# A fused recurrent-attention, expert and gated feed-forward kernel: two of eight pre-narrowed up-weight tiles move to the last stage, its second and third token groups start sooner, and its weight loads change queue

## The chip, the cores and the metric

The kernel runs on one core of a Trainium2 chip, in one launch. The metric is device microseconds (us) of one execution. Engines: PE (TensorE), DVE (VectorE), ACT (ScalarE), POOL (GpSimd) and SP (SyncE, which here only issues transfers). Each engine runs its instructions in the order in which they were written for it; semaphores tie the engines together.

## The reference

Three layers follow each other over 3072 tokens. The first is a gated recurrent attention (4 batches, 8 heads, 768 steps, head size 40), which gives rows of 320. The second sends each row to one of eight experts. The third, which the change is about, normalises each row and runs a gated feed-forward of width 1536:

```python
rms = np.sqrt(np.mean(x * x, axis=-1, keepdims=True) + 1e-06)
xn = x / rms * rms_g
g = xn @ w_gate                      # 320 -> 1536
silu = g * (1.0 / (1.0 + np.exp(-g)))
val = xn @ w_val                     # 320 -> 1536
return (silu * val @ w_out).astype(np.float32)
```

The weights of the third layer arrive as 64-bit floating point numbers.

## The kernel before, in words

**Stages.** Attention runs until about 220 us of the span, the expert stage from there to about 434 us, and the last stage to the end. All of it is written for the engines in one fixed order (`manual_schedule`), so the order below is the order on each engine.

**Number form.** Matmuls take 16-bit floats. A value is split into a high and a low 16-bit part, and products of the parts are summed. Weights of the last stage must first be *narrowed*: a 64-bit number is turned into a 32-bit one by five DVE instructions (`narrow`, L1263 to L1267, on 384 columns for an up tile and 320 for a down tile), ACT then scales it and rounds it to the high part, and the difference is the low part.

**Expert stage.** 28 blocks of 128 gathered rows. For block j, `xpose` (L1078) turns the gathered rows on the SP queue, `up` makes 16 matmuls (L1110), ACT and DVE split the result into h, SP turns h (L1118), and `down` makes 24 matmuls (L1142). The block after next is gathered by POOL. Beside this, `ffn_jobs` narrows some of the up weights of the last stage for later: per job one SP load (L1279, 384 KB), five DVE instructions, ACT and DVE for the two parts (L1294, L1301) and a store of the narrowed tile to DRAM (`UWS`, L1307). `UF` says how many of the 12 up tiles are done here, two jobs each (gate and value). `due` at L1162 says in which block each step of job k is written: its load in block 2 + floor(6k/5), and the rest in the four blocks behind. SP takes a job's load after the two turns of h, ahead of the next turn of x.

**Last stage.** Tokens come in six groups of 512 (n = 0 to 5), the up weights in 12 tiles (f). A *slot* is `upf(n, f)`: 16 matmuls of 128x512 into two PSUM banks (L1484), tanh on ACT (`th`, L1488), two DVE instructions (`u`, L1494 and L1495), the high part on ACT (`h`, L1499) and the low part on POOL (L1500). PSUM holds three slots: the banks of slot p are used again by slot p + 3. `plan` (L1531) is the list of slots: first groups 0, 1, 2 over the tiles f < UF, then f from UF on with the three groups in turn, then group 3 until its seventh tile, then the down matmuls of group 0 (`downf(0)`, L1517), and so on. With UF = 8 group 1 starts at slot 8, group 2 at slot 16, and `downf(0)` comes behind slot 42.

**A token group** is made ready in eight steps, placed beside slots by `beside` (L1538): step 5 `fetch` (four POOL gathers, L1334), steps 6 and 7 the sums of squares on ACT (L1349), with the norm on DVE and POOL (L1355, L1356) and the token numbers on POOL (L1361) behind 7, then steps 0 to 3: for 128 rows each, ACT scales (L1372, L1374), POOL subtracts (L1375) and copies (L1380), and SP turns the rows into `XT` (L1391).

**Narrowing in the last stage.** The other up tiles (f >= UF, eight jobs with UF = 8) and all 12 down tiles are narrowed beside the slots: `fill` is one list of small steps, seven to a job (five DVE steps, `high` on ACT, `low` on POOL), and each slot takes an equal share of the list (`at`), from slot 2 to slot 42, half ahead of the slot's two `u` instructions and half behind its `h`. The raw weights have three buffers; `low` of job k also issues the load of job k + 3 (`wload`, L1412), here on SP.

Of the kernel before, what the change touches and what calls it, by code (L numbers as in the profile page):

```python
# [11 lines left out]
I32 = mybir.dt.int32  # L12
# [23 lines left out]
OO = DM + H * 41  # L36
NEG = -1.0e30
FJ = (23, 24, 25)
UF = 8
HB = 43  # L40
TS = ((0, 7),), ((1, 1), (2, 3), (3, 5))
PARK = {6: 4, 4: 5, 5: 7}
# [32 lines left out]
class Net:  # L75
# [38 lines left out]
    def consts(self):  # L114
# [30 lines left out]
        self.MP = dp.tile([32, 3, S], BF, name="MP")  # L145
        self.UWS = dp.tile([UF, 128, 2, 5 * 128], F16, name="UWS")

# [940 lines left out]
    def moe(self):  # L1088
        nc, M, P = self.nc, self.M, self.P
# [69 lines left out]
        due = {}  # L1159
        for k, job in enumerate(jobs):  # L1160
            for step, (late, part) in zip(job, ((0, 1), (2, 0), (2, 1), (3, 0), (3, 1), (4, 0))):
                steps = due.setdefault((6 * k // 5 + late, part), [])  # L1162
                steps.insert(len(steps) * part, step)
        w2 = self.w2
        slot = [0]
# [77 lines left out]
    def ffn_weights(self):  # L1243
        self.UW = self.up.tile([128, NF, 2, 5, 128], F16, name="UW")
        self.XT = [self.up.tile([128, 4, 6, 128], F16, name=f"XT{i}") for i in range(4)]
        for f in range(UF):
            self.uw(f)
# [22 lines left out]
    def ffn_jobs(self):  # L1270
# [3 lines left out]
        def job(f, g):  # L1274
            st = {}

            def load():
                t = st["t"] = self.stg().bitcast(I32)
                nc.sync.dma_start(t[:, 0:768], self.i["wu"][f, g].bitcast(I32))  # L1279

            def some(lo, hi):
                def go():
                    if lo == 0:
                        st["v"], st["steps"] = self.narrow(st["t"], 384)
                    for step in st["steps"][lo:hi]:
                        step()

                return go

            def high():  # L1290
                of = st["of"] = st["t"][:, 0:320].bitcast(F16)
                for k in range(3):
                    c = slice(128 * k, 128 * k + 128)
                    nc.scalar.activation(of[:, c], st["v"][:, c], AF.Copy, scale=self.gs[:, k : k + 1])  # L1294

            def low():
                v, of = st["v"], st["of"]
                for k in range(3):
                    c, p = slice(128 * k, 128 * k + 128), slice(64 if k == 2 else 0, 128)
                    out = of[p, c] if k == 2 else of[:, 384 + 128 * k : 512 + 128 * k]  # L1300
                    nc.vector.scalar_tensor_tensor(  # L1301
                        out=out, in0=v[p, c], scalar=self.gs[p, k : k + 1], in1=of[p, c],
                        op0=ALU.mult, op1=ALU.subtract,
                    )

            def store():
                nc.scalar.dma_start(self.UWS[f, :, g], st["of"])  # L1307

            return load, some(0, 2), some(2, 5), high, low, store

        return [job(f, g) for f in range(UF) for g in range(2)]

# [82 lines left out]
    def ffn(self):  # L1395
        nc, F, P = self.nc, self.F, self.P
# [6 lines left out]
        fetch, norm1, norm2, flip = self.fetch, self.norm1, self.norm2, self.flip  # L1403
        todo = [(f, g) for f in range(UF, NF) for g in range(2)] + [(f, None) for f in range(NF)]
        raw = {}

        def wload(k):
            if k < len(todo):
                f, g = todo[k]
                src = self.i["wo"][128 * f : 128 * f + 128] if g is None else self.i["wu"][f, g]  # L1410
                t = F.tile([128, 768 + 384], F32, tag="wraw", bufs=3, name="wraw").bitcast(I32)
                nc.sync.dma_start(t[:, 0 : 2 * src.shape[-1]], src.bitcast(I32))  # L1412
                raw[k] = t

        def wjob(k):

            f, g = todo[k]
            st = []

            def narrow(i):  # L1420
                if i == 0:
                    st.extend(self.narrow(raw.pop(k), DM if g is None else 384))
                st[1][i]()

            def high():
                v = st[0]
                if g is None:
                    nc.scalar.activation(DW[:, f, 0], v, AF.Copy, scale=WSC)
                    nc.scalar.activation(v, v, AF.Copy, scale=WSC)
                    return  # L1430
                for i in range(3):
                    c = slice(128 * i, 128 * i + 128)
                    nc.scalar.activation(v[:, c], v[:, c], AF.Copy, scale=self.gs[:, i : i + 1])
                nc.scalar.activation(UW[:, f, g, 0:3].rearrange("p k c -> p (k c)"), v, AF.Copy)

            def low():
                v = st[0]
                sub = lambda out, a, b: nc.gpsimd.tensor_tensor(out, a, b, ALU.subtract)  # L1438
                if g is None:
                    sub(DW[:, f, 1], v, DW[:, f, 0])  # L1440
                else:
                    two = lambda a: a.rearrange("p k c -> p (k c)")
                    sub(two(UW[:, f, g, 3:5]), v[:, 0:256], two(UW[:, f, g, 0:2]))
                    tail = UW[64:128, f, g, 2]
                    sub(tail, v[64:128, 256:384], tail)
                wload(k + 3)

            return [lambda i=i: narrow(i) for i in range(5)], high, low
# [3 lines left out]
        for k in range(len(todo)):  # L1452
            n, high, low = wjob(k)
# [76 lines left out]
        run = lambda n, a, b: [(n, f) for f in range(a, b)]  # L1530
        plan = [x for n in range(3) for x in run(n, 0, UF)]  # L1531
        plan += [(n, f) for f in range(UF, NF) for n in range(3)]
        plan += run(3, 0, 7) + [(0,)] + run(3, 7, NF) + [(1,)] + run(4, 0, 3) + [(2,)]
# [1 line left out]
        order = [x for x in plan if len(x) == 2]  # L1535
        beside = {(0,): [[(4, 6)], [(4, 7), (4, 0)], [(4, 1), (4, 2)], [(4, 3)]]}
        beside[2,] = [[(5, k) for _, k in ks] for ks in beside[0,]]
        for n, p, steps in ((1, 0, (6, 7, 0, 1, 2, 3)), (2, 5, (5, None, None, 6, 7, 0, 1, 2, 3)), (3, 18, (5, None, None, 6, 7, 0, 1, 2, 3))):  # L1538
            for i, k in enumerate(steps):
                if k is not None:  # L1540
                    beside.setdefault(order[p + i], []).append((n, k))
        beside[3, 0], beside[3, 7] = [(4, 5)], [(5, 5)]
        fetch(1)
        for k in range(3):
            wload(k)
# [101 lines left out]
```

## Time and profile before

| what | value |
|---|---|
| time of three runs | 815.86 us median (813.55, 815.86, 821.99) |
| the profiled execution | 818.5 us, of which its span is 816.7 us |
| PE, DVE, ACT, POOL busy | 95%, 54%, 44%, 46% of the span |
| granted TensorE clock, mean | 0.963 of full speed |
| expert stage | from about 220 us to 434 us |
| last stage | from 434.25 us to the end |

The profile is one execution. "Busy" is the time in which an engine had an instruction in it, also one that was held up after its start. A wait is the idle time ahead of an instruction, with what ended it. PE is busy for 95% of the span, so the waits of PE, and what ends them, say where time can come from or go to. For the other engines the shares are averages over three stages with different work; the rows below give the last stage by itself.

### The profile page before, as it was taken

How to read it: one execution, taken by the hardware profiler on the slowest of the kernel's cores; microseconds unless marked ns; L12 is line 12 of the kernel's file. 1: busy time of each engine (PE TensorE's matmuls, PEld its weight loads, DVE VectorE, ACT ScalarE, POOL GpSimd, SP SyncE). 2: the span in 40 equal slices, each digit the busy share in tenths (PEclk: the TensorE clock that was granted, in tenths of full speed). 3: DMA queues.
4: the chain of work that ended last, by engine and by line, in shares of the span. 5: the costliest groups of instructions: out<-in, count | busy, mean ns of one | idle time of the engine just before them, and what ended most of it. 6: DMA issues, size and time to landing. Idle time of an engine off the chain costs nothing. (4 is left out here: it accounts for less than half of the span.)

```text
span 816.7 us, 15414 instructions
## 1 busy us (share of the span) xinstructions
PE 772.0 (95%) x5288; PEld 491.0 (60%) x5288; DVE 437.1 (54%) x874; ACT 357.8 (44%) x775; POOL 375.0 (46%) x445
## 2 busy tenths in 40 slices
PE   8999999998689999999899998999999999999993
PEld 7799998987245555555455444444565575544662
DVE  7658988885874645465223877778712112243010
ACT  4557878773422333233425664554432232233110
POOL 3537877862563323223424885765634232233221
PEclk9879999996889999999999999999999999999997
DMA  6567877864579999999875432242121020000000
GB/s 198 162 211 233 275 238 253 262 206 149 160 156 199 228 232 228 208 204 233 173 131 209 91 88 62 73 83 61 49 71 41 25 64 17 25 0 1 25 17 25
DMA packets 135573, 109.60 MB, mean 134 GB/s; under 512 B 107287, under 2 KB 116127, under 8 KB 135497
## 3 DMA queue, kind: packets, MB, share of 16 engines
q1 hardware_dynamic: 123561, 87.33, 43.5%
q0 software_dynamic: 5408, 13.83, 6.0%
q10 hardware_dynamic: 6528, 7.44, 2.9%
q8 instruction: 48, 0.79, 0.4%
q14 instruction: 28, 0.23, 0.1%
HBM read 67.59 MB, written 16.82 MB: 103 GB/s over the span
## 5 line engine op out<-in xcount | busy, mean ns | idle before, releaser
L1484 PE MATMUL gv<-XT,UW 128*128 128x512 f16 x1152 | 249.8, 379 | 2.8 <-DMA XT<-xr 2.8
L1484 PEld LDWEIGHTS <-UW 128*128 128x128 f16 x1152 | 112.7, 98 | 137.9 <-issue 3.2
L1494 DVE SCALAR_TENSOR_TENSOR u<-th,gv 128x512 f32<-128x512 f32 x72 | 49.4, 686 | 156.7 <-ACT th L1488 154.1
L1500 POOL TENSOR_TENSOR h<-u,h 128x512 f16<-128x512 f32 x72 | 84.8, 1180 | 105.4 <-ACT h L1499 104.9
L1517 PE MATMUL do<-DW,h 128*128 128x320 f16 x864 | 118.5, 299 | 0.9 <-POOL DW L1438 0.9
L1110 PE MATMUL ups<-W,xt 128*128 x448 | 105.8, 391 | 12.6 <-DMA xt<-xg 11.6
L1517 PEld LDWEIGHTS <-h 128*128 128x128 f16 x864 | 84.5, 98 | 34.8 <-issue 1.1
L1499 ACT ACTIVATE h<-u 128x512 f16<-128x512 f32 x72 | 45.4, 630 | 112.9 <-DVE u L1495 112.9
L1114 ACT ACTIVATE h<-ups 128x512 f16<-128x512 f32 x56 | 33.4, 597 | 124.9 <-PE ups L1110 103.5
L1142 PEld LDWEIGHTS <-hT 128*128 128x128 f16 x672 | 66.2, 99 | 32.5 <-issue 2.1
L1110 PEld LDWEIGHTS <-xt 128*128 128x128 f16 x448 | 44.8, 100 | 67.1 <-DMA xt<-xg 14.2
L1115 DVE SCALAR_TENSOR_TENSOR h<-ups,h 128x512 f16<-128x512 f32 x56 | 38.6, 691 | 85.2 <-ACT h L1114 43.9
L1070 POOL DMA_INDIRECT xg<-XD,IDX x28 | 28.8, 1029 | 97.9 <-DMA xt<-xg 92.8
L1522 POOL DMA_INDIRECT out_dram<-os,TKN x24 | 23.5, 980 | 80.2 <-ACT os L1520 76.7
L1495 DVE SCALAR_TENSOR_TENSOR u<-u,gv 128x512 f32<-128x512 f32 x72 | 49.5, 688 | 14.6 <-PE gv L1484 10.3
L488 PE MATMUL S<-QK 104*128 104x128 f32 x384 | 53.4, 284 | 1.7 <-DMA QK<-in_pqk_dram 1.7
L544 PEld LDWEIGHTS Y<-t,D 128*128 128x128 f32 x352 | 52.6, 204 | 3.7 <-issue 0.3
L544 PE MATMUL Y<-t,D 128*128 128x41 f32 x352 | 54.3, 259 | 0.0
L488 PEld LDWEIGHTS S<-QK 104*128 104x128 f32 x384 | 52.0, 201 | 3.3 <-issue 2.6
L1142 PE MATMUL dps<-W2A,hT 128*128 x336 | 51.2, 301 | 2.0 <-ACTq L1224 2.0
L1142 PE MATMUL dps<-W2B,hT 128*128 x336 | 51.6, 303 | 0.0
L1488 ACT ACTIVATE th<-gv 128x512 f32<-128x512 f32 x72 | 42.3, 587 | 17.0 <-PE gv L1484 17.0
(274 smaller groups left out, 1139.3 us busy)
## 6 DMA issues: line engine op xcount, KB each, us to landing
t<-in_pk_dram SPq DMA_DIRECT2D x22, 484.0 KB
QK<-in_pqk_dram SPq DMA_DIRECT2D x48, 160.0 KB
stg<-in_wu_dram SPq DMA_DIRECT2D x16, 384.0 KB
stg<-in_w_dram SPq DMA_DIRECT2D x9, 640.0 KB
XD<-xr SPq DMA_DIRECT2D x23, 192.0 KB
YD<-LG ACTq DMA_DIRECT2D x26, 160.5 KB
stg<-in_w_dram SPq DMA_DIRECT2D x8, 512.0 KB
wraw<-in_wo_dram SPq DMA_DIRECT2D x12, 320.0 KB
```

The lines of the kernel that those rows point to most:

```text
L488: nc.tensor.matmul(ps[:, i * L : (i + 1) * L], t["kz"][:, j, i], t["t1"][:, i], start=True, stop=True)
L544: nc.tensor.matmul(t["Y"][:, hp, 41 * hf : 41 * hf + 41], t["D"][hf][:, hp * L : (hp + 1) * L], t["vv"][:, 4 * hf + hp], start=False, stop ...
L1110: nc.tensor.matmul(ps, t["xt"][:, kx], self.W1[:, ds(o1 + (kw * F1 + f * 512), 512)], start=(n == 0), stop=(n == 7),)
L1115: nc.vector.scalar_tensor_tensor(out=h[:, 1], in0=ps, scalar=0.0, in1=h[:, 0], op0=ALU.max, op1=ALU.subtract)
L1142: nc.tensor.matmul(ps[:, 0:DM], hT[:, l, k % 4], r, start=(n == 0), stop=(n == 23))
L1484: nc.tensor.matmul(ps, UW[:, f, gv, kw], xt[:, :, 3 * hl + kx], start=(a == 0), stop=(a == 7))
L1488: nc.scalar.activation(th, pg, AF.Tanh, scale=0.5 / (XN * WSC))
L1494: nc.vector.scalar_tensor_tensor(out=u, in0=th, scalar=1.0, in1=pg, op0=ALU.add, op1=ALU.mult)
L1495: nc.vector.scalar_tensor_tensor(out=u, in0=u, scalar=1.0 / (XN * WSC) ** 2, in1=pv, op0=ALU.mult, op1=ALU.mult)
L1499: nc.scalar.activation(hh, u, AF.Copy)
L1500: nc.gpsimd.tensor_tensor(hl, u, hh, ALU.subtract)
L1517: nc.tensor.matmul(ps[:, 0:DM], l[:, s], DW[:, f, w], start=(a == 0), stop=(a == 3 * NF - 1))
```

## The change

Four edits: `UF` goes from 8 to 6, so 12 jobs instead of 16 are narrowed in the expert stage, and 24 instead of 20 in the last stage (12 up, 12 down; half of the 24 up jobs). The expert stage's jobs are spread as 2 + floor(3k/2). The loads of `wload` go from SP to POOL. And the steps of groups 1 and 2 are placed sooner, since group 1 now starts at slot 6 and group 2 at slot 12: group 1 has steps 6 and 7 at slot 0, 0 and 1 at slot 1, 2 at slot 2, 3 at slot 3; group 2 has its fetch at slot 2 and its last step at slot 9 (before: 5 and 13).

```diff
-UF = 8
+UF = 6
...
-                steps = due.setdefault((6 * k // 5 + late, part), [])
+                steps = due.setdefault((3 * k // 2 + late, part), [])
...
-                nc.sync.dma_start(t[:, 0 : 2 * src.shape[-1]], src.bitcast(I32))
+                nc.gpsimd.dma_start(t[:, 0 : 2 * src.shape[-1]], src.bitcast(I32))
...
-        for n, p, steps in ((1, 0, (6, 7, 0, 1, 2, 3)), (2, 5, (5, None, None, 6, 7, 0, 1, 2, 3)), (3, 18, (5, None, None, 6, 7, 0, 1, 2, 3))):
+        for n, p, steps in ((1, 0, (6, 0, 2, 3)), (1, 0, (7, 1)), (2, 2, (5, None, 6, 7, 0, 1, 2, 3)), (3, 18, (5, None, None, 6, 7, 0, 1, 2, 3))):
```

What this does to the order of instructions is shown at three places. The first is POOL at the start of the last stage, from the gathers of group 1 (`yg`) on. In a row stand the line, the operation, the tile written and those read. `h` is the low part of a slot, `nrm` the norm, `xr` the rows of a group, `UW` a narrowed up tile, `wraw` a raw weight. Before:

```order
L1334 DMA yg<-YD,RSLOT 128x321 x4
L1500 TENSOR_TENSOR h_5767<-u_5763,h_5766 128x512
L1500 TENSOR_TENSOR h_5797<-u_5793,h_5796 128x512
L1356 TENSOR_TENSOR nrm<-nrm,NH 128x4
L1361 COPY TKN<-yg 128x1 x4
L1375 TENSOR_TENSOR xr_5828<-yg,xr_5828 128x320
L1380 COPY xr_5828<-xr_5828 128x2x64
L1500 TENSOR_TENSOR h_5839<-u_5834,h_5838 128x512
L1375 TENSOR_TENSOR xr_5864<-yg,xr_5864 128x320
L1380 COPY xr_5864<-xr_5864 128x2x64
L1500 TENSOR_TENSOR h_5875<-u_5870,h_5874 128x512
```

Now (the rows from the third load on down to the last 128 rows of group 1):

```order
L1412 DMA wraw<-in_wu_dram 128x768 x3
L1500 TENSOR_TENSOR h_5709<-u_5705,h_5708 128x512
L1356 TENSOR_TENSOR nrm<-nrm,NH 128x4
...
L1375 TENSOR_TENSOR xr_5749<-yg,xr_5749 128x320
L1380 COPY xr_5749<-xr_5749 128x2x64
L1500 TENSOR_TENSOR h_5759<-u_5755,h_5758 128x512
L1375 TENSOR_TENSOR xr_5782<-yg,xr_5782 128x320
L1380 COPY xr_5782<-xr_5782 128x2x64
L1500 TENSOR_TENSOR h_5794<-u_5788,h_5793 128x512
L1334 DMA yg<-YD,RSLOT 128x321 x4
L1375 TENSOR_TENSOR xr_5827<-yg,xr_5827 128x320
L1380 COPY xr_5827<-xr_5827 128x2x64
```

Three loads now stand behind the gathers of group 1, and the four gathers of group 2 stand ahead of the last rows of group 1; before they stood behind them.

The second place is POOL some slots later, where only slots (`h`) and up tiles are left. Before:

```order
L1500 TENSOR_TENSOR h_6328<-u_6323,h_6327 128x512
L1438 TENSOR_TENSOR UW<-wraw,UW 128x256
L1438 TENSOR_TENSOR UW<-wraw,UW 64x128
L1500 TENSOR_TENSOR h_6362<-u_6356,h_6361 128x512
L1500 TENSOR_TENSOR h_6395<-u_6390,h_6394 128x512
```

Now:

```order
L1500 TENSOR_TENSOR h_6149<-u_6143,h_6148 128x512
L1438 TENSOR_TENSOR UW<-wraw,UW 128x256
L1438 TENSOR_TENSOR UW<-wraw,UW 64x128
L1412 DMA wraw<-in_wu_dram 128x768
L1500 TENSOR_TENSOR h_6183<-u_6177,h_6182 128x512
L1438 TENSOR_TENSOR UW<-wraw,UW 128x256
L1438 TENSOR_TENSOR UW<-wraw,UW 64x128
L1412 DMA wraw<-in_wu_dram 128x768
```

Up tiles come at nearer to two in three slots than one in two, and each brings a load on POOL.

The third place is SP in the middle of the expert stage (`xt`: turned rows of a block, `hT`: turned h, `stg`: a raw up weight, `YD<-zero`: a store of zeros). Before:

```order
L1197 DMA YD<-zero_73 384x1x107
L1279 DMA stg<-in_wu_dram 128x768
L1078 DMA_TRANSPOSE xt<-xg 128x6x128
L1118 DMA_TRANSPOSE hT<-h 128x8x128 x2
L1279 DMA stg<-in_wu_dram 128x768
L1078 DMA_TRANSPOSE xt<-xg 128x6x128
L1118 DMA_TRANSPOSE hT<-h 128x8x128 x2
L1197 DMA YD<-zero_73 384x1x107
L1279 DMA stg<-in_wu_dram 128x768
L1078 DMA_TRANSPOSE xt<-xg 128x6x128
```

Now:

```order
L1197 DMA YD<-zero_73 384x1x107
L1279 DMA stg<-in_wu_dram 128x768
L1078 DMA_TRANSPOSE xt<-xg 128x6x128
L1118 DMA_TRANSPOSE hT<-h 128x8x128 x2
L1279 DMA stg<-in_wu_dram 128x768
L1078 DMA_TRANSPOSE xt<-xg 128x6x128
L1118 DMA_TRANSPOSE hT<-h 128x8x128 x2
L1197 DMA YD<-zero_73 384x1x107
L1078 DMA_TRANSPOSE xt<-xg 128x6x128
```

Four of the 16 loads ahead of a turn of x are gone; here it is the one of the tenth block.

## Rows read from the trace of the kernel before

**Rows 1.** Waits of PE, whole span: waiter, releaser: total us, times, longest.

```profile
PE ups L1110 <- DMA xt<-xg: 11.6, 7, 2.9
...
PE do L1517 <- POOL DW L1438: 0.9, 1, 0.9
```

**Rows 2.** Timeline of PE: start us, us, line, count [idle before and its end].

```profile
251.95 3.62 PE L1110 MATMUL ups<-W,xt 128*128 x16
...
385.90 3.62 PE L1110 MATMUL ups<-W,xt 128*128 x16
...
392.61 2.25 PE L1110 MATMUL ups<-W,xt 128*128 x9
...
434.25 55.42 PE L1484 MATMUL gv<-XT,UW 128*128 128x512 f16 x256
492.44 47.86 PE L1484 MATMUL gv<-XT,UW 128*128 128x512 f16 x221 [2.78 <-DMA XT<-xr]
```

**Rows 3.** Stretches: us, then busy us (count) of PE, PEld, DVE, ACT, POOL; clock, DMA.

```profile
242.00:249.00 7.00, 6.64 (x19) 2.54 (x20) 2.52 (x9) 0.70 (x2) 2.85 (x3) 0.56 0.86 171
...
434.00:592.00 158.00, 154.35 (x731) 71.25 (x729) 117.09 (x189) 89.36 (x198) 106.25 (x125) 1.00 0.31 80
```

**Rows 4.** Groups of POOL in 434 to 592 us: busy us, mean ns | idle before.

```profile
L1334 POOL DMA_INDIRECT yg<-YD,RSLOT x15 | 15.0, 1000 | 4.1 <-issue 4.1
L1375 POOL TENSOR_TENSOR xr<-yg,xr 128x320 f16<-128x320 f32 x12 | 10.6, 887 | 4.8 <-ACT yg L1374 4.8
...
L1438 POOL TENSOR_TENSOR UW<-wraw,UW 128x256 f16<-128x256 f32 x8 | 7.1, 889 | 0.0
...
L1380 POOL COPY xr<-xr 128x128 f16<-128x128 f16 x12 | 4.7, 394 | 0.8
L1438 POOL TENSOR_TENSOR UW<-wraw,UW 64x128 f16<-64x128 f32 x8 | 4.1, 510 | 1.1 <-DMA yg<-YD,RSLOT 0.5
```

**Rows 5.** Narrowing of 384 columns in the expert stage: ns min/median/max, first and last start.

```profile
L1263 DVE TENSOR_SCALAR stg<-stg x16: 349/350/352, 255.5 to 382.3; 128x384 int32<-128x384 int32 x16
L1264 DVE SCALAR_TENSOR_TENSOR stg<-stg x16: 558/559/560, 255.8 to 382.7; 128x384 int32<-128x384 int32 x16
L1265 DVE SCALAR_TENSOR_TENSOR stg<-stg x16: 548/557/560, 256.9 to 384.1; 128x384 int32<-128x384 int32 x16
L1266 DVE TENSOR_SCALAR stg<-stg x16: 354/356/559, 257.4 to 384.5; 128x384 int32<-128x384 int32 x16
L1267 DVE SCALAR_TENSOR_TENSOR stg<-stg x16: 557/558/560, 257.8 to 385.1; 128x384 f32<-128x384 int32 x16
```

**Rows 6.** Timelines of DVE, then of POOL, at one narrowing instruction and later another.

```profile
571.37 0.48 DVE L1265 SCALAR_TENSOR_TENSOR wraw<-wraw 128x320 int32<-128x320 int32 x1
...
576.77 4.45 DVE L1265 SCALAR_TENSOR_TENSOR wraw<-wraw 128x320 int32<-128x320 int32 x1
...
570.85 1.03 POOL L1334 DMA_INDIRECT yg<-YD,RSLOT  x1 [0.16 <-issue]
...
575.98 1.17 POOL L1500 TENSOR_TENSOR h<-u,h 128x512 f16<-128x512 f32 x1
...
580.08 0.78 POOL L1438 TENSOR_TENSOR DW<-wraw,DW 128x320 f16<-128x320 f32 x1
```

**Rows 7.** Timeline of DVE: the first `u` of slot 15 and of slot 42.

```profile
495.24 0.69 DVE L1494 SCALAR_TENSOR_TENSOR u<-th,gv 128x512 f32<-128x512 f32 x1 [1.94 <-ACT th L1488]
...
587.28 0.69 DVE L1494 SCALAR_TENSOR_TENSOR u<-th,gv 128x512 f32<-128x512 f32 x1
```

**Rows 8.** Timeline of POOL: slot 0, the norm of group 1, the last rows of group 2.

```profile
439.86 1.15 POOL L1500 TENSOR_TENSOR h<-u,h 128x512 f16<-128x512 f32 x1 [2.43 <-ACT h L1499]
...
445.55 1.10 POOL L1356 TENSOR_TENSOR nrm<-nrm,NH 128x4 f32<-128x4 f32 x1
...
489.02 0.50 POOL L1380 COPY xr<-xr 128x128 f16<-128x128 f16 x1
```

**Rows 9.** Timeline of POOL at the program's start: a plain load that POOL issued.

```profile
4.94 0.62 POOL L176 DMA_DIRECT2D cst<-in_cst_dram  x1
```

## The prediction

> **What bounds the kernel now.** I read the waits of PE first, since PE is busy 95% of the span. Two places matter. In the expert stage PE waits 11.6 us for turned rows [rows 1]. In the last stage it hardly waits at all: 2.78 us for the turned rows of group 2 [rows 2] and 0.9 us for the last down weight [rows 1]. So the last stage is a row of matmuls without gaps, and anything that runs beside it is free as long as it stays hidden. The question is how well it is hidden, and for that I read the stretches and POOL's groups of the last stage, and then the timelines of DVE and POOL against each other.
>
> A slot lasts 55.42 / 16 = 3.46 us (256 matmuls, 16 a slot), so slot p starts at 434.25 + 3.46p [rows 2]. PSUM lets PE run three slots ahead, 10.4 us: the first `u` of a slot, which frees its bank 0.69 us after its start, may begin at most 9.7 us after the slot's start. Slot 15 starts at 486.2 and its `u` at 495.24 [rows 7]: 9.0 us behind. Slot 42 starts at 492.44 + 26 x 3.46 = 582.5 [rows 2] and its `u` at 587.28 [rows 7]: 4.8 us. So DVE is already most of the allowed distance behind, although it is busy for only 117 of the 158 us from 434 to 592 [rows 3].
>
> The reason is in the timelines. A narrowing instruction of 320 columns took 0.48 us under a gather that POOL issued at 570.85, and 4.45 us from 576.77 on, while POOL ran tensor instructions back to back from 575.98 until 580.08 + 0.78 = 580.86; it ended 0.36 us after the last of them [rows 6]. A narrowing instruction on DVE and a tensor instruction on POOL don't run together here; one waits for the other. An issued transfer on POOL does not hold DVE up. So the pair of them is one resource, and its load has to be added up.
>
> **The change, part by part.** *The pair in the last stage.* Without POOL beside it (expert stage), narrowing 384 columns takes 0.350 + 0.559 + 0.557 + 0.356 + 0.558 = 2.4 us by the medians [rows 5]; for 320 columns I take 2.0 us, an estimate by columns. Before, 8 up and 12 down jobs need 8 x 2.4 + 12 x 2.0 = 43 us of DVE. POOL's tensor work is 106.25 busy less 15.0 of gathers [rows 3, 4] = 91 us. Together 134 us, in the 152 us between the first low part at 439.86 [rows 8] and 592: 88% full, without much room, since the slots force an order on it.
> The change adds four up jobs between the same two ends (slot 2 to 42): each 2.4 us on DVE and 0.889 + 0.510 = 1.4 us on POOL [rows 4], 15.2 us in all. Then 150 of 152 us would have to be full. If the lost share stays as it is, the stretch grows by 15.2 x 152 / 134 = 17.2 us. Bounds: if the pair could be packed without loss, nothing is added (150 < 152); if also every load on POOL takes its time from the pair, 24 x 0.62 us [rows 9] = 14.9 us more, 32 us. I take 17.2: the loads stay out because a narrowing instruction can run under an issued transfer [rows 6], and because nothing in the order makes the pair denser. ACT gets 4 jobs more too, which lie in its idle time: 89 of 158 us busy [rows 3].
> How this reaches PE: the matmuls of a slot wait for the bank (the 9.7 us above), and `downf(0)` waits for the last down weight. With DVE at that limit at slot 42, 4.9 us later than now, the wait ahead of the down matmuls goes from 0.9 to about 6 us.
>
> *The token groups.* These waits are the same backlog seen at two other places, so I add nothing for them, but they show where it bites first. Group 1 must be turned 8 - 6 = 2 slots sooner, at 434.25 + 6 x 3.46 = 455.0. POOL's order from the first low part to its last copy holds three low parts (1.15), the norm (1.10) [rows 8], four gathers of 19.1 / 15 = 1.27, and four pairs of 0.887 + 0.394 [rows 4]: 14.8 us. From 439.86 that ends at 454.6 without a pause. The turn and its landing take 492.44 - 489.52 = 2.9 us from the end of the copy [rows 2, 8], so 457.5: a wait of 2.5 us at least. If the norm starts no sooner than now, at 445.55, what is behind it gives 445.55 + 1.1 + 5.1 + 5.1 + 2.3 + 2.9 = 462.0, a wait of 7.0 us. I expect 4: group 1's gathers now queue behind six tile loads instead of eight, and the three raw loads come behind them, so the norm should start some us sooner than now. Group 2 keeps its distance of three slots between last step and use, so its wait of 2.8 us stays or grows a little.
>
> *The expert stage.* From 251.95 to 392.61 lie 20 blocks of 392.61 - 385.90 = 6.71 us undisturbed [rows 2]: 134.2 of 140.7 us, so 6.5 us of the waits for turned rows lie where jobs run. 4 of 16 loads, with their stores, go: 4/16 x 6.5 = 1.6 us gained. Bounds: nothing (the turns of h and x stay), and all 6.5. I take 1.6, since the other loads stay where they are in SP's order. The work that leaves DVE and ACT here was never waited for by PE.
>
> *The queue of the loads.* SP loses 20 issues; nothing waited for SP's issue time. On POOL an issue costs 0.62 us [rows 9], and none of the 24 lands ahead of a wait of PE: its raw tile is used more than a job later. It is a cost only through the pair, above.
>
> *Clock.* After a wait of 2.78 us the granted clock stayed at 2.4 GHz (the stretch 434 to 592 is at 1.00), but in 242 to 249 us, behind waits in the expert stage, it was at 0.56 on average, mostly 1.2 GHz [rows 3]. A half-clock piece after the wait of group 1 is possible; PE would catch up on work that the pair delays anyway, so I add 0, with up to 3 us in the range.
>
> **Sum.** 818.5 + 17.2 - 1.6 = 834.1 us against the profiled execution's own time. That execution is 2.6 us above the median of the runs, 815.86, so the forecast is 831 us.
>
> **The rivals.** *The pair packs better.* DVE may get its turn after the one POOL instruction that is running, rather than after a whole run of them; then 150 of 152 us can be filled and only the wait of group 1 is new: 815.9 + 4 - 1.6 - up to 2.8 (the wait of group 2) = 815 to 818 us. Against it: the 4.45 us [rows 6] span POOL instructions from 576.77 to 580.86, more than one. For it: PE hardly waits now at 88%. It decides if the `u` of slot 42 is no later than now.
> The Trainium skill, SBUF — State Buffer, section Who interferes with whom, has the lock between DVE with two SBUF inputs and GpSimd held "for the whole instruction". By that rule alone a held-up instruction waits for one POOL instruction and the time is this rival's; the trace agrees on the lock, but with 4.45 us not on its length.
>
> *Faster: SP was what held the groups up.* The SP queue takes a raw load ahead of some turns, and each load waits for POOL's `low`. If turns are late for that, taking the loads off SP frees 2.78 + 0.9 us [rows 1, 2], and with all 6.5 us of the expert stage 815.9 - 10.2 = 806 us. Against it: the last turn of group 2 lands 2.9 us after its copy, about what a turn takes anyway. It decides if the wait at group 2 goes and none comes at group 1.
>
> *Slower still: POOL's loads are held up too.* If DVE holds up POOL's issues, each of the 24 costs more than 0.62 us. By the rows a gather took 1.000 us on average beside narrowing and 1.03 at 570.85 [rows 4, 6], so a few tenths at most: 24 x 0.3 = 7 us more, 838 us.
> The same page, in the section SBUF: two separate sides, warns that a DMA issued by GpSimd cannot write its descriptors while DVE is in a two-port mode, with 620 ns alone and some 3100 ns beside a copy. By that an estimate would be 24 x 2.5 = 60 us more; the gathers above show no such stretch here.
>
> **Chances.** Forecast 0.62, slower still 0.13, better packing 0.17, faster 0.08. A change of 1%, 8 us, is about what a measurement of this kernel can tell. Faster by over 1% (below 807.7) comes from the SP rival alone: 0.08. Within 1%: better packing, 0.17. Slower by over 1% (above 824.0): 0.75. The range from 817 to 841 takes in half of the packing rival and the case of held-up loads; it leaves out the SP rival, the rest of the packing one and the upper bound of 32 us.
>
> **What would show it.** Right: a wait of about 4 us at slot 6 for XT, one of 3 us or more at slot 12, then small waits of PE for `u` over slots 15 to 41, narrowing instructions of several us, and a wait of about 6 us for DW ahead of the down matmuls; waits for xt down by 1 to 2 us. Wrong: `u` of slot 42 no later than 5 us after its slot, or no wait for DW. The forecast fails most easily on the loss in the pair, which I carried over from one stretch, and on the start of the norm of group 1.

## The result, and the profile after

The changed kernel takes 824.87 us (median of 8 runs) against 816.39 us (8 runs): a ratio of 1.0104, 95% interval 1.0069 to 1.0139, so some 6 to 11 us slower. The forecast of 831 us was 6 us too high. The two profiled executions differ by less, 820.79 against 818.5 us, because stages that the change doesn't touch vary from one execution to the next (the stretch up to the first expert matmul took 215.4 to 225.1 us in the profiled executions of the 14 kernels of this document). So the traces are read stage by stage, by the matmuls of PE that begin and end each stage:

| stage (profiled execution) | before | after | difference |
|---|---|---|---|
| up to the first expert matmul | 223.8 us | 220.2 us | -3.6 (not touched by the change) |
| expert stage | 210.4 | 206.9 | -3.5 (see below: not shown to be the change's) |
| last stage, first up to last down matmul | 370.1 | 386.1 | +16.0 |
| last matmul to the end of the span | 12.3 | 5.8 | -6.6 |

The last two rows give +9.4 us, which agrees with the measured ratio. The prediction had +17.2 for the one and no term for the other.

The waits of PE after (columns as in [rows 1]):

```profile
PE ups L1110 <- DMA xt<-xg: 10.0, 6, 3.7
PE gv L1484 <- DMA XT<-xr: 5.3, 1, 5.3
PE gv L1484 <- DVE u L1494: 4.2, 4, 1.8
...
PE do L1517 <- POOL DW L1438: 2.4, 2, 1.2
```

The line for XT is now the wait at slot 6; it was 2.78 us at slot 16 [rows 2], and slot 12 has none. The waits for `u` are new. The down weights show again in the timeline of PE, split over two releasers (POOL's low part and ACT's high part):

```profile
427.12 20.88 PE L1484 MATMUL gv<-XT,UW 128*128 128x512 f16 x96
453.26 68.41 PE L1484 MATMUL gv<-XT,UW 128*128 128x512 f16 x304 [5.26 <-DMA XT<-xr]
522.38 3.61 PE L1484 MATMUL gv<-XT,UW 128*128 128x512 f16 x16 [0.70 <-DVE u L1494]
527.51 14.28 PE L1484 MATMUL gv<-XT,UW 128*128 128x512 f16 x64 [1.52 <-DVE u L1494]
543.54 41.72 PE L1484 MATMUL gv<-XT,UW 128*128 128x512 f16 x192 [1.75 <-DVE u L1494]
585.52 3.61 PE L1484 MATMUL gv<-XT,UW 128*128 128x512 f16 x16 [0.26 <-DVE u L1494]
588.97 4.24 PE L1517 MATMUL do<-DW,h 128*128 128x320 f16 x30
593.57 0.43 PE L1517 MATMUL do<-DW,h 128*128 128x320 f16 x2 [0.36 <-ACT DW L1428]
595.20 0.30 PE L1517 MATMUL do<-DW,h 128*128 128x320 f16 x1 [1.20 <-POOL DW L1438]
597.14 0.43 PE L1517 MATMUL do<-DW,h 128*128 128x320 f16 x2 [1.65 <-ACT DW L1428]
598.76 6.48 PE L1517 MATMUL do<-DW,h 128*128 128x320 f16 x35 [1.19 <-POOL DW L1438]
```

The waits add up to 5.3 + 4.2 + 4.4 = 13.9 us, against 2.8 + 0.9 = 3.7 before: 10.2 of the 16.0 us. Most of the rest is in the durations. 304 matmuls took 68.41 us, where 304 at the 55.42 / 256 us of [rows 2] are 65.8: 2.6 us more. The stretches say why (columns as in [rows 3]):

```profile
453.00:459.00 6.00, 5.74 (x15) 2.12 (x16) 2.25 (x5) 4.55 (x12) 4.68 (x10) 0.53 0.20 66
459.00:521.00 62.00, 62.00 (x289) 28.11 (x288) 56.02 (x78) 34.70 (x79) 45.86 (x56) 1.00 0.30 80
...
588.00:605.00 17.00, 12.61 (x76) 7.78 (x74) 7.63 (x15) 7.87 (x20) 9.10 (x14) 0.90 0.04 12
605.00:813.00 208.00, 208.00 (x1260) 123.06 (x1258) 43.76 (x66) 50.49 (x95) 62.50 (x67) 1.00 0.10 29
```

Behind the wait at slot 6 the granted clock was mostly at its lower level, 1.2 GHz (0.53 on average), then full again. Behind the waits for the down weights it was 0.90; from the first down matmul to the last it takes 813.2 - 589.0 = 224.3 us (218.7 before), 5.6 us more, of which 4.4 - 0.9 = 3.5 are waits, and about 2 are left for the clock.

DVE shows what the jobs met (groups of DVE from 415 to 610 us: busy us, mean ns of one | idle before, releaser):

```profile
L1264 DVE SCALAR_TENSOR_TENSOR wraw<-wraw 128x384 int32<-128x384 int32 x12 | 12.1, 1010 | 0.3
...
L1263 DVE TENSOR_SCALAR wraw<-wraw 128x320 int32<-128x320 int32 x12 | 5.8, 484 | 6.9 <-DMA wraw<-in_wo_dram 6.9
```

A two-input instruction that took 0.56 us in the expert stage [rows 5] takes 1.01 here, so POOL holds DVE up, as forecast. But DVE also stood idle for 6.9 us for raw down loads (1.0 us before), which the prediction did not expect. The longest, 5.6 us until 584.29, is told by POOL:

```profile
574.97 1.04 POOL L1334 DMA_INDIRECT yg<-YD,RSLOT  x1 [0.17 <-issue]
...
579.93 0.81 POOL L1438 TENSOR_TENSOR DW<-wraw,DW 128x320 f16<-128x320 f32 x1
581.04 0.60 POOL L1412 DMA_DIRECT2D wraw<-in_wo_dram  x1 [0.30 <-POOL DW L1438]
```

Four gathers of group 3, from 574.97 on, stand ahead of a low part; the load behind that part is issued at 581.04, and DVE has its data 3.2 us later. With it `u` goes from 5.2 us behind its slot at slot 38 to 10.1 us at slot 39, shortly ahead of the down matmuls. It looks like a cost of the loads on POOL, but experiment 1 shows that it isn't.

The end of the program is in no list of busy engines: it is a sequencer instruction. The closing instructions of POOL's queue (ns min/median/max, first and last start us), before:

```profile
L1642 POOLq DRAIN  x3: 46/109/10417, 805.4 to 816.4; - x3
```

and after:

```profile
L1642 POOLq DRAIN  x3: 46/109/3857, 814.3 to 818.7; - x3
```

POOL's drain behind its last scatter took 10.42 us before and 3.86 after. That is the 6.6 us.

### The profile page after: what moved, and what is told of

Its sections match the earlier page's. It is cut to its first block, busy times and chain, and to the rows that moved or that the text cites. A ratio compares the mean times of both kernels' runs of the same rounds, so it can differ in the third digit from the quotient of the medians.

```text
span 819.0 us, 15377 instructions
## 1 busy us (share of the span) xinstructions
PE 771.8 (94%) x5286; PEld 489.1 (60%) x5288; DVE 440.2 (54%) x862; ACT 360.0 (44%) x779; POOL 394.4 (48%) x477
## 5 line engine op out<-in xcount | busy, mean ns | idle before, releaser
L1484 PE MATMUL gv<-XT,UW 128*128 128x512 f16 x1152 | 253.3, 382 | 9.6 <-DMA XT<-xr 5.3
L1500 POOL TENSOR_TENSOR h<-u,h 128x512 f16<-128x512 f32 x72 | 87.3, 1215 | 93.3 <-ACT h L1499 92.8
L1517 PE MATMUL do<-DW,h 128*128 128x320 f16 x864 | 120.5, 301 | 4.4 <-POOL DW L1438 2.4
L1110 PE MATMUL ups<-W,xt 128*128 x448 | 103.3, 384 | 11.4 <-DMA xt<-xg 10.0
L1495 DVE SCALAR_TENSOR_TENSOR u<-u,gv 128x512 f32<-128x512 f32 x72 | 49.5, 688 | 15.2 <-PE gv L1484 10.4
L544 PEld LDWEIGHTS Y<-t,D 128*128 128x128 f32 x352 | 50.9, 198 | 3.4
```

What stands on the lines that cost most here:

```text
L544: nc.tensor.matmul(t["Y"][:, hp, 41 * hf : 41 * hf + 41], t["D"][hf][:, hp * L : (hp + 1) * L], t["vv"][:, 4 * hf + hp], start=False, stop ...
L1110: nc.tensor.matmul(ps, t["xt"][:, kx], self.W1[:, ds(o1 + (kw * F1 + f * 512), 512)], start=(n == 0), stop=(n == 7),)
L1484: nc.tensor.matmul(ps, UW[:, f, gv, kw], xt[:, :, 3 * hl + kx], start=(a == 0), stop=(a == 7))
L1495: nc.vector.scalar_tensor_tensor(out=u, in0=u, scalar=1.0 / (XN * WSC) ** 2, in1=pv, op0=ALU.mult, op1=ALU.mult)
L1500: nc.gpsimd.tensor_tensor(hl, u, hh, ALU.subtract)
L1517: nc.tensor.matmul(ps[:, 0:DM], l[:, s], DW[:, f, w], start=(a == 0), stop=(a == 3 * NF - 1))
```

## Experiments

Two theories stood at the start. **The pair**: DVE's narrowing and POOL's tensor work exclude each other, and 15.2 us more of it in a fixed time is the cost. **The rival**: the loads on POOL, or the order of the groups, carry it. "Last stage" is always from the first up to the last down matmul of one profiled execution.

**1. Loads back on SP** (changed kernel, one line).

```
-  nc.gpsimd.dma_start(t[:, 0 : 2 * src.shape[-1]], ...)
+  nc.sync.dma_start(t[:, 0 : 2 * src.shape[-1]], ...)
```

> The changed kernel with its raw loads issued by SP again; six narrowed tiles and the new order of the token groups stay. The last stage runs from the first up matmul to the last down matmul (386.1 us in the changed kernel, 370.1 before). Theory of the pair (narrowing on DVE and tensor work on POOL exclude each other, and 15.2 us more of it is what costs): the 6.9 us that DVE waited for raw loads go, but the pair stays as full, so 383 to 386 us and 822 to 825 us in all. Rival, the loads (a load issued by POOL starts only when POOL has worked off what is ahead of it, and DVE stands idle meanwhile): up to 7 us come back, 379 us, and 818 us in all.

Measured: last stage 381.8 us, between the two theories; the end of the program 12.3 us again; ratio to before 1.011 (1.003 to 1.019). The waits of PE:

```profile
PE gv L1484 <- DMA XT<-xr: 6.2, 1, 6.2
PE do L1517 <- POOL DW L1438: 2.2, 2, 1.2
...
PE gv L1484 <- DVE u L1494: 0.3, 1, 0.3
```

With the loads on SP the waits for `u` go from 4.2 to 0.3 us, while those for the down weights stay (3.8 us, 4.4 in the changed kernel). So POOL's loads cost 4.3 us of the 16.0, and give 6.6 back at the end of the program.

What they cost is not DVE's idle time for raw data. The first narrowing instruction (groups of DVE from 415 to 610 us), in the changed kernel and then with the loads on SP:

```profile
L1263 DVE TENSOR_SCALAR wraw<-wraw 128x384 int32<-128x384 int32 (+1 forms) x24 | 13.6, 568 | 7.4 <-DMA wraw<-in_wo_dram 6.9 <-DMA wraw<-in_wu_dram 0.4
...
L1263 DVE TENSOR_SCALAR wraw<-wraw 128x384 int32<-128x384 int32 (+1 forms) x24 | 12.2, 509 | 9.4 <-POOL DW L1438 5.0 <-DMA wraw<-in_wo_dram 3.8 <-DMA wraw<-in_wu_dram 0.6
```

With the loads on SP this idle time is longer, 9.4 us, and 5.0 of it lie at the same place as the 5.6 us: the load needs a raw buffer that the same low part, behind the same four gathers, sets free. What the loads on POOL lengthen is the narrowing itself: the five instructions of the 24 jobs take 81.3 us of DVE with the loads on POOL and 73.8 with the loads on SP. Why is not shown. A load on POOL takes 0.56 us and moves POOL's tensor work behind it to a later time, so that it can meet other narrowing instructions; that is an argument and no measurement.

**2. The queue alone** (kernel before, the same line the other way).

> The kernel before with one edit alone: its 20 raw loads are issued by POOL. Theory of the pair: nothing (last stage 370 to 372 us, 816 us in all), since a narrowing instruction runs on under an issue. Rival, the loads: DVE's waits for raw loads, 1.0 us before, rise to 5 us or more, u of slot 42 comes later than 5.1 us behind its slot, and the last stage takes 373 to 378 us.

Measured: ratio 0.9931 (0.9889 to 0.9973), so 0.7% faster: neither theory had that. Last stage 372.4 us, 2.3 more: a wait of 4.1 us at slot 16 with a slower clock behind it. End of the program 5.6 us, with a drain of 3.69. That is 2.3 - 6.7 = -4.4 us by stages, and 806.5 against 812.0 us by the medians.

**3. The groups alone** (kernel before, with the changed tuple in the loop over `n, p, steps`).

```
-  (1, 0, (6, 7, 0, 1, 2, 3)), (2, 5, (5, None, None, 6, 7, ...
+  (1, 0, (6, 0, 2, 3)), (1, 0, (7, 1)), (2, 2, (5, None, 6, 7, ...
```

> The kernel before with one edit alone: groups 1 and 2 are fetched and turned in the changed kernel's slots, while eight up tiles stay narrowed in the expert stage, so that the groups are used at slots 8 and 16 as before. Theory of the pair: no new wait; the 2.8 us wait of group 2 goes or shrinks, 367 to 371 us for the last stage, 813 to 816 us in all. Rival, the order (group 2's four gathers stand on POOL ahead of group 1's last rows, and the waits that follow cost more than they show): a wait at slot 8 and 3 to 6 us more, 373 to 376 us.

Measured: no wait at slot 8 and none at slot 16, but 3.4 us in five waits for `u` and 1.8 for the down weights; last stage 375.4 us. With the steps done sooner `u` lies 9.7 us behind its slot at slot 8 (3.1 before), and the wait for the turn becomes one for `u`. In the time the 5 us don't show: ratio 1.0011 (0.9974 to 1.0048), the one run in which time and last stage disagree by more than the interval.

**4. Group 2's gathers behind group 1's last rows** (changed kernel).

```
-  (2, 2, (5, None, 6, 7, 0, 1, 2, 3))
+  (2, 3, (5, None, 6, 0, 1, 2, 3)), (2, 5, (7,))
```

> The changed kernel with group 2's gathers, and the steps behind them except the last norm step and its squares, one slot later, so that POOL does the last rows of group 1 ahead of the gathers (four gathers, 4 x 1.27 = 5.1 us). Theory of the pair: the wait at slot 6 goes from 5.3 to about 0.5 us and the clock stays at 2.4 GHz behind it, but the pair is as full as it was, so that the waits for u and for the down weights grow by most of that: last stage 383 to 386 us. Rival, the order: the wait and the slower clock behind it (5.3 + 2.6 us) were a loss by themselves, and the last stage takes 378 to 380 us, 817 us in all.

By the edit only the gathers (slot 2 to 3) and step 6 (slot 4 to 5) come later; steps 0 to 3 of group 2 stay in slots 6 to 9.

Measured: last stage 386.1 us, as in the changed kernel; ratio to before 1.0087 (1.0037 to 1.0138). Its timeline of PE:

```profile
425.16 41.60 PE L1484 MATMUL gv<-XT,UW 128*128 128x512 f16 x192
473.73 50.43 PE L1484 MATMUL gv<-XT,UW 128*128 128x512 f16 x224 [6.96 <-DMA XT<-xr]
```

The first row has 192 matmuls, twelve slots: slot 6 doesn't wait any more. Slot 12 does, for 6.96 us, with 1.9 us of slower clock behind it. A row of gathers moved, and its wait with it.

**5. The pair by itself** (appended behind the last matmul of the kernel before; `t1` and `t2` are free tiles).

```
+            "subtract": [lambda: nc.gpsimd.tensor_tensor(c2, a2, b2, ALU.subtract)] * 6,
...
+                ops = self.narrow(t1.bitcast(I32), 383)[1]
...
+                for d in dve:
+                    ops[d]()
```

> The kernel before with a measurement appended behind its last matmul, on free tiles: DVE runs eight two-input narrowing instructions of 383 columns and then eight one-input ones, once beside an idle POOL and once each beside back-to-back POOL subtractions (128x512), copies, fills and plain load issues; each stretch starts when both engines are free. The span grows by the appended work and is not the point. Theory of the pair: beside the subtractions a two-input instruction can't finish while POOL goes from one to the next, so that eight of them take as long as the subtractions and themselves together (6 x 1.15 + 8 x 0.56 = 11.4 us), and one-input ones too (6.9 + 8 x 0.35 = 9.7 us); beside issues they take what they take alone (4.5 and 2.8 us). Rival, that only one POOL instruction is waited for: DVE and POOL take turns, which gives the same sums but with every DVE instruction spread evenly (each about 1.7 us) and no single one above 1.8 us. Rival, no lock at all between them: 0.56 and 0.35 us throughout.

Measured (ns min/median/max; L1265 has two inputs, L1263 one), two-input instructions alone, then one-input and two-input ones beside subtractions, then two-input ones beside issues:

```profile
L1265 DVE SCALAR_TENSOR_TENSOR wb<-wb x8: 547/557/557, 801.7 to 805.8; 128x383 int32<-128x383 int32 x8
...
L1263 DVE TENSOR_SCALAR wb<-wb x7: 359/1199/1334, 806.4 to 813.1; 128x383 int32<-128x383 int32 x7
L1562 POOL TENSOR_TENSOR wb<-wb x6: 1145/1155/1155, 806.8 to 813.0; 128x512 f16<-128x512 f32 x6
...
L1265 DVE SCALAR_TENSOR_TENSOR wb<-wb x8: 558/1391/1528, 814.8 to 824.0; 128x383 int32<-128x383 int32 x8
L1562 POOL TENSOR_TENSOR wb<-wb x6: 1148/1346/1348, 815.3 to 822.2; 128x512 f16<-128x512 f32 x6
...
L1265 DVE SCALAR_TENSOR_TENSOR wb<-wb x8: 549/557/557, 852.2 to 856.3; 128x383 int32<-128x383 int32 x8
L1565 POOL DMA_DIRECT2D wb<-in_wo_dram x6: 546/572/620, 852.0 to 856.9; - x6
```

They take turns, one for one, so the rival was right here: no DVE instruction takes above 1.53 us. A round of a subtraction and a two-input instruction lasts 1.39 us ((822.24 - 815.31) / 5 between starts of subtractions), not 1.15 + 0.56 = 1.71: adding the two up is some 20% too dear. Beside issues the two-input instructions take what they take alone, and an issue takes 0.55 to 0.62 us; but POOL pauses for 2.0 us between the fourth and the fifth issue, and what ends that pause the profile doesn't say. The 4.45 us of [rows 6] are another case, and POOL's timeline before shows it: 575.98 + 1.17 = 577.15 lies behind the next start, 577.10, and so on until 580.86. In the appended loop POOL leaves 0.08 us after each subtraction, in that stretch nothing. A missing gap doesn't decide by itself, though. In the traces of all kernels but experiment 8's, take the narrowing instructions that lasted 0.2 us or more beyond their time alone. Wherever POOL left a gap (0.06 us or more) such an instruction got its turn. Where the next POOL instruction had started ahead of the end of the one before, it got its turn 107 times, and 38 times it was passed over though it had been waiting for 0.1 us or more. What decides there, no run tells.

**6. The four extra jobs left empty.** Their loads and slots stay, their narrowing and low parts go, and ACT makes two copies for a job in place of three scalings and a rounding (values of tiles 6 and 7 left out).

```
+                    if light:
+                        st[:] = [UW[:, f - 6, g, 0:3].rearrange("p k c -> p (k c)"), [lambda: None] * 5]
...
+                if light:
+                    nc.scalar.activation(UW[:, f, g, 3:5], UW[:, f - 6, g, 3:5], AF.Copy)
```

> The changed kernel, in which the jobs of the four extra up weights (tiles 6 and 7) keep their loads, their slots and their ACT work, but neither narrow on DVE nor subtract on POOL: ACT copies another tile's weights in their place, so the values of tiles 6 and 7 are left out. That takes 4 x (2.4 + 1.4) = 15.2 us from the pair. Theory of the pair: the waits for u and for the down weights (4.2 + 4.4 us) go, and the last stage falls from 386.1 to about 376 us, where the wait at slot 6 and the slower clock behind it stay; a little less if slot 6 gains too. Rival, the order and the queue (sooner groups and POOL's loads carry the cost): 382 us or more.

Measured: 383.1 us, only 3.0 less. This is the run against the pair theory as the prediction used it: of 15.2 us of work only 3.0 came back. The waits of PE hardly change:

```profile
PE gv L1489 <- DMA XT<-xr: 4.1, 1, 4.1
PE gv L1489 <- DVE u L1499: 3.2, 3, 1.8
PE do L1522 <- POOL DW L1441: 2.1, 2, 1.2
```

The four jobs stand first in the list, in slots 2 to 8, and the waits for `u` come at slots 25 to 30. From slot 26 to slot 42 `u` lies as far behind its slot as in the changed kernel, to 0.1 us: what was taken out early is no help later.

**7. The four extra jobs gone from the list**, so that 20 jobs are spread over the 41 slots from 2 to 42, as before.

```
-  todo = [(f, g) for f in range(UF, NF) for g in range(2)] + ...
+  todo = [(f, g) for f in range(UF + 2, NF) for g in range(2)] + ...
```

> The changed kernel, in which the jobs of the four extra up weights are gone from the list (ACT copies two other tiles in their place at the start, so the values of tiles 6 and 7 are left out): 20 jobs spread over slots 2 to 42 as before, groups and POOL's loads as changed. Taking the work of the same four jobs away but leaving their slots gave only 3.0 us. Theory that the jobs a slot has to take decide (24 over 40 slots against 20): u of slots 24 to 42 lies as far behind as before (8.9 us at most, 5 at slot 42), no wait for u, about 1 us for the down weights, and only the wait at slot 6 with its slower clock is left: 370.1 + 4 + 2 - 2.8 = 373 to 375 us. Theory that the queue of loads and the order of the groups cost the rest: as with the jobs left empty, 381 to 384 us.

Measured: 376.5 us, 9.6 less than the changed kernel:

```profile
PE gv L1484 <- DMA XT<-xr: 5.5, 1, 5.5
...
PE do L1517 <- POOL DW L1438: 1.3, 1, 1.3
PE gv L1484 <- DVE u L1494: 0.3, 1, 0.3
```

The waits for `u` are gone, that for the down weights is near the 0.9 of before, and `u` of slot 42 lies 5.5 us behind its slot (5.1 before, 9.1 in the changed kernel). What differs from experiment 6 is the slots: there the other 20 jobs had to be done in what the first four left. (Four loads on POOL are gone too, but all 24 cost 4.3 us in experiment 1, so four of them can't be the 6.6 us between the two runs.) So the jobs a slot must take decide, 24 over 41 slots against 20, and not the total of the stage. What is left over before, 6.4 us, is mostly slot 6: 5.5 - 2.8 of wait and 2.6 of clock. With experiment 2 this makes a row of single steps: 370.1 before, 372.4 with the loads on POOL, 376.5 with the groups used and made sooner as well, 386.1 with the four jobs too. In this order the queue costs 2.3 us, the groups 4.1 and the four jobs 9.6.

**8. Fills in place of h's subtraction** (changed kernel; the low part of `h` is left out).

```
-  nc.gpsimd.tensor_tensor(hl, u, hh, ALU.subtract)
+  nc.gpsimd.memset(u, 0.0)
+  nc.gpsimd.memset(u[:, 0:256], 0.0)
```

> The changed kernel, in which POOL fills u with a constant behind ACT's rounding instead of subtracting (two fills in about the same time), and the matmuls of the low part read the high part again: the low part of h is left out, everything waits as before. Theory of the pair, if a fill doesn't exclude DVE: the narrowing instructions of 384 columns fall from 3.94 us a job to near the 2.4 us they take alone, the waits for u and the down weights go, and the last stage takes 376 to 379 us. If POOL's order alone is what delays (loads, low parts and groups behind each other), POOL is as busy as before and the last stage stays above 383 us.

Measured: last stage 376.8 us, no wait for `u`; a job of 384 columns takes 2.78 us of DVE, where it took 3.94. It doesn't separate as cleanly as meant: the fills took 0.54 + 0.33 = 0.87 us against 1.25 for the subtraction, so POOL had 16 us less to do as well. That fills let two-input instructions pass is shown by the appended loop of experiment 5 (557 ns each beside fills of 0.53 us).

**9 to 11. How many loads on POOL** (kernel before): the first three, the last three (`k >= 17`), the first ten (`k < 10`).

```
+  (nc.gpsimd if k < 3 else nc.sync).dma_start(...)
```

> The kernel before with the first three of its 20 raw loads issued by POOL, the others by SP. It is about the end of the program: from the last matmul to the end of the span it took 12.3 us in all three kernels whose raw loads SP issued, and 5.6 to 5.8 us in all three that issued them on POOL; POOL's last drain makes up the difference. Theory that POOL's drain depends on whether it ever issued plain loads: 5.7 us here too. Theory that it depends on how many transfers POOL issued: 12.3 us, or something between. Last stage 370 to 371 us either way.

> The kernel before with the last three of its 20 raw loads issued by POOL, the others by SP. POOL's drain at the end took 10.42 us with none on POOL, 10.66 with the first three, 3.69 with all 20 and 3.86 with 24. If it is the number of transfers that POOL issued, 10.7 us as with the first three. If it is what kind of transfer POOL issued late, 3 to 4 us. Last stage 369 to 371 us either way.

> The kernel before with the first ten of its 20 raw loads issued by POOL, the others by SP. If POOL's drain at the end goes by the number of transfers that POOL issued, it grows on slowly from 10.66 us (three) to about 11 or drops to 3 to 4 us at some number between three and twenty; if it goes by how late the last plain load was, about 10.5 us here and 3 to 4 us with the last three. Last stage 369 to 372 us.

Measured, POOL's drain at the end: 10.66 us with the first three, 10.66 with the last three, 3.29 with the first ten. The last stages took 369.1, 370.4 and 373.0 us. With the other kernels this orders by count alone: 10.42 with none (three kernels), 10.66 with three, 3.29 with ten, 3.68 to 3.70 with 20 (three kernels), 3.85 to 3.87 with 24 (four). With three it doesn't matter which they are: first or last give the same. It grows slowly with the count and drops by some 7 us between three and ten. The kernel of experiment 5, with six smaller loads some 50 us behind its last scatter, has a drain of 2.82 us, which fits a drop between three and six, but its loads come at another place. Why it drops, no run tells.

**12. The best of it**: the kernel before with POOL's loads and group 2's steps behind its gathers one slot sooner.

```
-  (2, 5, (5, None, None, 6, 7, 0, 1, 2, 3))
+  (2, 5, (5, None, 6, 7, 0, 1, 2, 3))
```

> The kernel before with its 20 raw loads on POOL and group 2's squares, norm and turns one slot sooner behind its gathers (eight up tiles narrowed in the expert stage, as before). With the loads alone on POOL the last stage took 372.4 us, with a wait of 4.1 us at slot 16 and 1.5 us more in that slot under a lower clock, and the end of the program 5.6 instead of 12.3 us. If the turned rows are what slot 16 waits for, both go, unless slots 11 to 15, where u lay 8.6 to 10.5 us behind, now wait for u: last stage 367 to 370 us, in all 0.7 to 1.4% faster than before. If the denser steps only move the wait from the turn to u (as in the kernel with the sooner groups alone, 3.4 us), 371 to 373 us and no gain over the kernel with POOL's loads alone, 0.7%.

Measured: 0.9888 of before (0.9834 to 0.9943), so faster than both kernels. Last stage 371.7 us: the wait for the turn shrinks from 4.1 to 1.4 us, and 2.2 for `u` take its place, as the second case had it. Against the queue alone (0.9931) nothing is shown, since the intervals overlap.

## Why the prediction was right and wrong, point by point

- **Direction**: right, and 824.9 us lies in the range. The 6 us by which the forecast is too high are about one missing term, the end of the program.
- **What failed: "the queue of the loads" at no cost.** Both halves were wrong. The step is "the loads stay out" of the pair. On POOL they cost 4.3 us of the last stage (experiment 1): the same narrowing takes 81.3 us of DVE instead of 73.8, and PE waits 4.2 us for `u` instead of 0.3. "None of the 24 lands ahead of a wait of PE" was not so either, since DVE's 5.6 us without data make the down weights late; but that is not the queue, as DVE idles 9.4 us ahead of its first narrowing instruction with the loads on SP and 7.4 with them on POOL. How the loads lengthen the narrowing stays open. It is no fixed price: with 20 loads on POOL narrowing took 66.0 us in experiment 2 and 62.3 in experiment 12, against 63.7 before. And the loads save 6.6 us at the end of the program, in a drain that the profile before showed as 10.4 us behind the last scatter. I had read nothing of the span behind the last matmul.
- **The pair, 17.2 us**: the last stage grew by 16.0, but not as argued. A total of 150 in 152 us says little, because each job has its slot: taking out the extra work without its slots gave 3.0 us, with its slots 9.6. DVE and POOL overlap in part too (1.39 for 1.71 us). The four jobs cost 9.6 of the 16.0 us; the groups and the queue, for which the sum had nothing, the rest (experiment 7). That the size came out near is chance.
- **The token groups**: slot 6 waited 5.3 us (forecast 4), slot 12 not at all (forecast 3). These waits are not "the same backlog seen at two other places": with 20 jobs in the list the wait at slot 6 was still 5.5 us. It is a cost of its own. Moving the gathers (experiment 4) only moved it.
- **DW**: 4.4 us against a forecast of 6; `u` of slot 42 lay 9.1 us behind its slot, forecast near 9.7. Right in place and near in size, but not by a backlog that had built up: at slot 38 `u` was only 5.2 us behind, and the jump to 10.1 at slot 39 is DVE's 5.6 us without raw data, behind group 3's gathers. This is read from the traces; no run moves those gathers. (Before, `u` of slot 42 lay 5.1 us behind; the 4.8 of the prediction took an estimated start of the slot.)
- **Clock**: forecast 0, up to 3. It was 2.6 behind slot 6 and about 2 at the first down matmuls. Waits and clock together, 10.2 + 2.6 + 2 = 14.8 of the 16.0 us, leave nothing for a catching up.
- **Expert stage, -1.6**: not shown. With all 16 jobs it took 204.1 to 210.6 us (mean 207.7, eight executions), with 12 jobs 204.9 to 213.1 (mean 209.5, six). The -3.5 of the first two traces lies within that spread.
- **The rivals.** Faster, SP held the groups up: not so, a wait at slot 6 came, and with the loads on SP it was longer, 6.2 us against 5.3. Loads held up by DVE's narrowing: not seen, the 24 issues of the changed kernel took 0.56 to 0.63 us each, 0.62 alone [rows 9]. The Trainium skill, SBUF — State Buffer, section SBUF: two separate sides, expects issues to be drawn out beside a two-port DVE mode; the appended loop had issues beside two-input instructions only, and there an issue took 0.57 us. Better packing: DVE often gets its turn after one POOL instruction (the loop, and 107 of 145 times without a gap), but not always. The same page's "for the whole instruction" (section Who interferes with whom) fits experiment 5 but for an overlap of some 0.32 us a round, and does not account for the 4.45 us by itself.

## What to carry to other kernels

Work that is tied to slots is budgeted by the slot, not by the stage: see what one slot must take, and which engine that waits in turn. A transfer that is moved to a busy engine's queue shifts that engine's other work, so ask whom that work holds up, not only who waits for the data. And a wait that the changed kernel shows is the change's only if it goes when the edit is taken back: DVE's 5.6 us without data stayed. Read the span behind the last matmul too: 12 us were lying there, and a change of queue took half of them.

## What was not expected of the hardware

- POOL's closing drain takes 10.4 to 10.7 us in programs with up to three more transfers on POOL and 3.3 to 3.9 us with ten to 24 more; with three it doesn't change by their place. The cause stays open.
- DVE and POOL alternate instruction by instruction where POOL leaves gaps of 0.08 us (1.39 us a round). Where POOL leaves none, DVE got its turn 107 times and was passed over 38 times, at most for a run of POOL instructions and 4.45 us.
- A fill on POOL leaves two-input DVE instructions at 557 ns, but stretches one-input ones from 0.36 to 0.64 us.
- After waits of PE for turned rows of 4.0 to 7.0 us (eight kernels) the clock fell to its lower level for some microseconds each time, at 1.5 to 2.6 us of loss; after waits of 1.4, 1.8 and 2.8 us at slot 16 it did not.
